# The remainder of a down product: one 96-row matmul per token tile and a last tile of 384 and 128 columns, in place of 32-row packing and a last tile of 256 and 256

## The chip, the cores and the metric

The kernel runs on one core of a Trainium2 chip. The metric is the device time of one execution in microseconds, lower is better. The time before is the median of three runs.

## What is computed

The kernel is a SwiGLU feed-forward layer in bf16:

```python
B, S, D, F = 1, 2048, 512, 1376
# x (B, S, D), w_gate (D, F), w_up (D, F), w_down (F, D)
def reference(x, w_gate, w_up, w_down):
    g = _silu(x @ w_gate)
    u = x @ w_up
    return (g * u) @ w_down
```

F is 1376 = 10 x 128 + 96. The hidden dimension is the contraction dimension of the down product, so each token tile needs ten full 128-row matmuls there and a remainder of 96 rows. That remainder is what the change is about.

## The kernel before

**Layout.** x is loaded transposed (xT_sb: D on partitions in KD = 4 blocks, tokens along the free dimension). The tokens are worked on in four chunks of 512 (NSC = 4), each of four tiles of 128 tokens (TPC = 4), sixteen tiles in all (NST = 16). The hidden activations hT_sb hold hidden rows on partitions, tokens along the free dimension, in NFF = 10 full blocks of 128 rows. PSUM is eight banks of 512 fp32 columns.

**Order of the work.** A small planner (`_Plan`) keeps one list of operations for each engine, in the order in which the code calls `op` and `dma`. Each operation names the operations that it depends on. At the end each list is written out, and a wait on a semaphore is put ahead of an operation where its dependency is on another engine; a wait for a count that the engine has already waited for is left out. A semaphore counts the finished operations of an engine, so waiting for one operation means waiting for all that stand before it in that engine's list. There is no other scheduling: each engine runs its list in order.

**Gate and up product (lines 172 to 194).** For every chunk and each of the ten full hidden blocks, TensorE does four matmuls for the gate into one of three banks (psG, banks 0 to 2) and four for up into one of two (psU, banks 3 and 4), all from `mm_k`, L172. ScalarE (ACT) takes the silu of the gate bank (L191), VectorE (DVE) multiplies it by the up bank and writes a 128 x 512 bf16 block of hT_sb (L194). `last_mult[c]` is the last such product of a chunk.

**The 96 remaining hidden rows** come in two blocks. Block X is one more set of four matmuls per chunk (also L172): its 128 output rows in bank 5 (psX) are the 96 gate rows and the last 32 up rows. ACT takes the silu of both parts (L222 and L223). Block Y is the first 64 up rows; it is done after all four chunks, two chunks side by side in the two column halves of the array (L232, 16 matmuls with a `tile_position`), into banks 6 and 7 (psY).

DVE then multiplies gate by up. Before the change this is done by `scatter` (L202): the 96 rows are cut into three groups of 32 rows (j) and each into four pieces of 128 tokens (r). Piece r goes to partitions 32r to 32r + 31 of hr_sb, so that the four token tiles of a chunk lie in four different 32-partition strips. Group 2 (from block X) is scattered chunk by chunk (`rest_x`), groups 0 and 1 (from block Y) after the last chunk (`rest_y`): 48 products of 32 x 128 in all, 32 of them at the end.

**Down product.** Chunks are taken in pairs. `main_pass` (L250) does the ten full matmuls of a token tile. `rest_pass` (L265) does the remainder of a whole chunk: for each of three groups, four matmuls of 32 rows, each in its own row strip of the array (`tile_position`) and into its own bank. The order on TensorE for a pair of chunks is: four main passes of the first chunk into banks 0 to 3, the rest pass of the first chunk (it closes those banks), the rest pass of the second chunk into banks 4 to 7 (it opens them), and four main passes of the second chunk. The 96 remainder rows of w_down are loaded four times, once to each strip (wdr_sb).

**Output.** `put` copies a bank to one of four o_sb buffers as bf16, on DVE (L284) or ACT (L282), and stores it (L286). The last of the sixteen tiles is done as two main passes of 256 columns (HD): the first in bank 7, copied by ACT and stored from ACT's queue, the second in bank 0, added by DVE to the part that the rest pass had left in bank 7 (part_sb, L300 and L279) and stored from SP's queue. All other stores and nearly all loads are issued by SP.

The first ten matmuls (L169) are there to warm TensorE up while the first loads arrive.

Of the kernel before, what the change touches and what calls it, by code (L numbers as in the profile page):

```python
# [4 lines left out]
ACT = mybir.ActivationFunctionType  # L5
ALU = mybir.AluOpType
BF16 = mybir.dt.bfloat16
# [11 lines left out]
class _Plan:  # L19
# [18 lines left out]
    def dma(self, eng, fn, deps=()):  # L38
        o = _Op(eng, fn, [d for d in deps if d is not None], False, self.sem(f"s_dma{self.n_dma}"))
        self.n_dma += 1  # L40
        self.lists[eng].append(o)
        return o
# [25 lines left out]
def bass_standalone__swiglu_ffn__prompt_kernel(nc, x, w_gate, w_up, w_down, out):  # L68
# [8 lines left out]
    NSC = S // SC  # L77
    TPC = SC // P
    NST = S // P
    HD = D // 2  # L80
    Q = 32
    assert D == 512 and S % SC == 0 and KD == 4 and TPC == 4 and F_LAST == 96 and NSC == 4

    xf = x[0]
# [7 lines left out]
    with ExitStack() as es:  # L92
# [3 lines left out]

        xT_sb = sb("xT_sb", [P, KD, S], BF16)
        w_sb = sb("w_sb", [P, KD, 2 * F], BF16)
        wd_sb = sb("wd_sb", [P, NFF, D], BF16)
        wdr_sb = sb("wdr_sb", [P, 3, D], BF16)  # L100
        hT_sb = sb("hT_sb", [P, NFF, S], BF16)
        hr_sb = sb("hr_sb", [P, 3, NSC, P], BF16)
        adummy = sb("act_dummy", [P, 8], FP32)
        NSG = 3
        sg_sb = [sb(f"sg_sb{i}", [P, SC], FP32) for i in range(NSG)]
        sgx_sb = [sb(f"sgx_sb{c}", [P, SC], FP32) for c in range(NSC)]
        sgy_sb = [sb(f"sgy_sb{c}", [P, SC], FP32) for c in range(NSC)]
        NOS = 4
        part_sb = sb("part_sb", [P, D], FP32)
        o_sb = [sb(f"o_sb{i}", [P, D], BF16) for i in range(NOS)]  # L110

        banks = [ps(f"bank{i}", [P, 512], FP32) for i in range(8)]
        NG, NU = 3, 2
        psG, psU, psX, psY = banks[0:3], banks[3:5], banks[5], banks[6:8]

        ones_w = nc.const_aps.tensor(1.0, [P, P], BF16)
        ones_m = nc.const_aps.tensor(1.0, [P, SC], BF16)
# [34 lines left out]
        for c in range(1, NSC):  # L152
            o = load_x("sp", c)
            for dk in range(KD):
# [1 line left out]
        got_wd = [  # L156
            dma("sp", lambda e: e.dma_start(
                wd_sb[:, 0:NFF, :], w_down[0:NFF * P, :].rearrange("(k p) d -> p k d", p=P))),
        ] + [
            dma("sp", lambda e, r=r: e.dma_start(  # L160
                wdr_sb[r * Q:(r + 1) * Q, :, :], w_down[NFF * P:F, :].rearrange("(j p) d -> p j d", p=Q)))
            for r in range(TPC)
        ]

        op("act", lambda e: e.activation(adummy[:, 0:4], zero_c, ACT.Silu), inc=False)  # L165
# [31 lines left out]
        def yblk(c):  # L197
            return (0, 64) if c % 2 == 0 else (64, 128)

        def scatter(c, j, sg, up, p0, deps):  # L200
            for r in range(TPC):
                o = op("dve", lambda e, r=r: e.tensor_tensor(  # L202
                    hr_sb[r * Q:(r + 1) * Q, j, c, :], sg[p0:p0 + Q, r * P:(r + 1) * P],
                    up[p0:p0 + Q, r * P:(r + 1) * P], ALU.mult), deps)
            return o

        n = 0
        rest_x, rest_a, last_mult = {}, {}, {}
        for c in range(NSC):
            ft0 = 0  # L210
            for ft in range(ft0, NFF):
                for dk in range(KD):
                    g = mm_g(n, c, ft, dk)
                for dk in range(KD):
                    u = mm_u(n, c, ft, dk)
                evac(n, c, ft, g, u)
                n += 1
            last_mult[c] = mults[-1]
            for dk in range(KD):
                xm = mm_k(psX, XC0, c, dk, [got_g[NFT - 1, dk], got_ut, rest_x.get(c - 1)])  # L220
            y0, y1 = yblk(c)
            op("act", lambda e, c=c: e.activation(sgx_sb[c][96:128, :], psX[64:96, :], ACT.Silu), [xm], inc=False)  # L222
            rest_a[c] = op("act", lambda e, c=c, y0=y0, y1=y1: e.activation(  # L223
                sgy_sb[c][y0:y1, :], psX[0:64, :], ACT.Silu), [xm])
            rest_x[c] = scatter(c, 2, sgx_sb[c], psX, 96, [rest_a[c]])

        rest_y = {}
        for pi in range(NSC // 2):
            for dk in range(KD):
                for c in (2 * pi, 2 * pi + 1):  # L230
                    y0, y1 = yblk(c)
                    ym = op("pe", lambda e, pi=pi, dk=dk, c=c, y0=y0, y1=y1: e.matmul(  # L232
                        psY[pi][y0:y1, :], lhsT=w_sb[:, dk, YC0:YC0 + 64], rhs=xT_sb[:, dk, c * SC:(c + 1) * SC],
                        start=(dk == 0), stop=(dk == KD - 1), tile_position=(0, y0), skip_group_check=True),
                        [got_u[NFT - 1, dk]], inc=(dk == KD - 1 and c % 2 == 1))
            for c in (2 * pi, 2 * pi + 1):
                y0, y1 = yblk(c)
                for j in range(2):
                    rest_y[c] = scatter(c, j, sgy_sb[c], psY[pi], y0 + j * Q, [rest_a[c], ym])


        stores = {}
        freed = {id(b): o for b, o in zip(banks, [[silus[-1]]] * NG + [[mults[-1]]] * NU + [[rest_x[NSC - 1]]] + [
            [rest_y[1]], [rest_y[NSC - 1]]])}

        def main_pass(t, bank, c0, ncol, opened):
            c = t // TPC
            for fk in range(NFF):
                deps = got_wd[0:1] + [last_mult[c]] + freed.get(id(bank), []) if fk == 0 else []
                om = op("pe", lambda e, fk=fk: e.matmul(  # L250
                    bank[:, c0:c0 + ncol],
                    lhsT=hT_sb[:, fk, t * P:(t + 1) * P], rhs=wd_sb[:, fk, c0:c0 + ncol],
                    start=(fk == 0 and not opened), stop=(fk == NFF - 1 and (opened or c0 > 0)), skip_group_check=True),
                    deps, inc=(fk == NFF - 1))
            return om

        def rest_pass(c, bank0, opening):
            for j in range(3):
                for r in range(TPC):
                    deps = []  # L260
                    if j == 0:
                        deps = got_wd[1:] + [rest_x[c], rest_y[c]]
                        if opening:
                            deps += freed.get(id(banks[bank0 + r]), [])
                    om = op("pe", lambda e, j=j, r=r: e.matmul(  # L265
                        banks[bank0 + r][:, :], lhsT=hr_sb[r * Q:(r + 1) * Q, j, c, :],
                        rhs=wdr_sb[r * Q:(r + 1) * Q, j, :], start=(opening and j == 0),
                        stop=(j == 2 and not opening), tile_position=(r * Q, 0), skip_group_check=True),
                        deps, inc=(j == 2 and r == TPC - 1))
            return om  # L270

        nout = 0

        def put(t, bank, c0, ncol, om, eng, q, part=None):
            nonlocal nout
            ob = o_sb[nout % NOS]
            prev = stores.get(nout - NOS, [])
            if part is not None:
                cp = op("dve", lambda e: e.tensor_tensor(  # L279
                    ob[:, c0:c0 + ncol], bank[:, c0:c0 + ncol], part_sb[:, c0:c0 + ncol], ALU.add), [om, part] + prev)  # L280
            elif eng == "act":
                cp = op("act", lambda e: e.activation(ob[:, c0:c0 + ncol], bank[:, c0:c0 + ncol], ACT.Copy), [om] + prev)  # L282
            else:
                cp = op("dve", lambda e: e.tensor_copy(ob[:, c0:c0 + ncol], bank[:, c0:c0 + ncol]), [om] + prev)  # L284
            freed.setdefault(id(bank), []).append(cp)
            stores.setdefault(nout, []).append(dma(q, lambda e: e.dma_start(  # L286
                of[t * P:(t + 1) * P, c0:c0 + ncol], ob[:, c0:c0 + ncol]), [cp]))
            if c0 + ncol == D:
                nout += 1

        for c in range(0, NSC, 2):
            for r in range(TPC):
                main_pass(c * TPC + r, banks[r], 0, D, False)
            om = rest_pass(c, 0, False)
            om2 = rest_pass(c + 1, TPC, True)
            for r in range(TPC):
                freed.pop(id(banks[r]), None)
                put(c * TPC + r, banks[r], 0, D, om, ("dve", "act")[r % 2], "sp")
            if c + 1 == NSC - 1:
                part = op("act", lambda e: e.activation(part_sb[:, HD:D], banks[7][:, HD:D], ACT.Copy), [om2])  # L300
            for r in range(TPC):
                t = (c + 1) * TPC + r
                bank = banks[TPC + r]
                freed.pop(id(bank), None)
                if t < NST - 1:
                    put(t, bank, 0, D, main_pass(t, bank, 0, D, True), "dve", "sp")
                else:
                    freed[id(bank)] = [part]
                    put(t, bank, 0, HD, main_pass(t, bank, 0, HD, True), "act", "act")
                    put(t, banks[0], HD, HD, main_pass(t, banks[0], HD, HD, False), "dve", "sp", part)  # L310
        for e in ("sp", "act"):
            plan.lists[e].append(_Op(e, None, [s for k in range(NST - NOS, NST) for s in stores[k] if s.eng == e], False))

        block = es.enter_context(nc.Block(no_gpsimd_drain=True))

# [43 lines left out]
```

## Time and profile before

| | us |
|---|---|
| median of 3 runs | 123.64 (123.58 to 123.75) |
| the profiled execution, its own time | 123.64 |
| its span, first to last instruction | 121.9 |
| TensorE matmul busy | 117.4 |
| DVE busy | 49.1 |
| ACT busy | 32.7 |
| granted TensorE clock (mean) | 1.000 |

The span is what the profile sees; what lies between it and the time of the execution is start and end of the program. Engines run side by side, so a busy time says what an engine did and not what set the end. A matmul's listed duration runs from its start to its modelled end, and matmuls overlap, so the pace of a stream has to be taken from the distance of starts. The loads are all in by about 28 us; the gate and up product runs to 78.2 us, block Y to 80.05 us, and the down product fills the rest.

### The profile page before, as it was taken

To read this page: it belongs to the slowest core of one execution; us is meant where nothing else is said; L and a number is where in the kernel's file an instruction comes from. 1 tells how busy PE (TensorE), PEld (TensorE's weight loads), DVE (VectorE), ACT (ScalarE), POOL (GpSimd) and SP (SyncE) were. 2 spreads that over 40 slices of the span, in tenths; PEclk is the share of its full clock that TensorE was granted. 3 is DMA by queue.
4 is the path that set the end of the run, shared out by engine and by line. 5 is a ranking of instruction groups with operands and counts; after the bars stand their busy time and mean duration, and the time that the engine had idled before them with its cause. 6 is when DMAs were issued, how large, how long until landed. Compare 5 with 4: busy or idle time off the path is not lost.

```text
span 121.9 us, 1487 instructions
## 1 busy us (share of the span) xinstructions
PE 117.4 (96%) x580; PEld 52.4 (43%) x580; DVE 49.1 (40%) x100; ACT 32.7 (27%) x56; POOL 0.2 (0%) x4
## 2 busy tenths in 40 slices
PE   7999999999999999999999999999969999999991
PEld 2244444444444444444444444444414444444470
DVE  0024433464433464424373443388893322004421
ACT  4033233353233353233443323400030000004010
POOL 0000000000000000000000000000000000000000
PEclk9999999999999999999999999999999999999999
DMA  4999999940000000000000000000005121003312
GB/s 85 253 285 375 263 231 264 337 85 0 0 0 0 0 0 5 0 0 5 0 0 0 0 0 0 5 0 0 0 0 172 48 86 43 0 0 113 102 53 76
DMA packets 18326, 8.80 MB, mean 72 GB/s; under 512 B 11408, under 2 KB 18320, under 8 KB 18320
## 3 DMA queue, kind: packets, MB, share of 16 engines
q1 hardware_dynamic: 17648, 8.52, 26.2%
q10 hardware_dynamic: 672, 0.20, 0.7%
q8 instruction: 4, 0.07, 0.2%
q14 instruction: 2, 0.02, 0.0%
HBM read 4.52 MB, written 2.10 MB: 54 GB/s over the span
## 4 chain that ended last, share of the span: by engine, by line
PE 87%; DVE 9%; issue 1%; ACT 1%
PE bank L172 60%; PE bank L250 21%; DVE hr_sb L202 8%; PE bank L169 4%; PE bank L265 2%; ACT sgy_sb L223 0%; ACT sgx_sb L222 0%; DVE o_sb L279 0%
## 5 line engine op out<-in xcount | busy, mean ns | idle before, releaser
L172 PE MATMUL bank<-xT_sb,w_sb 128*128 128x512 bf16 x336 | 73.1, 380 | 0.0
L172 PEld LDWEIGHTS bank<-xT_sb,w_sb 128*128 128x128 bf16 x336 | 32.9, 98 | 40.6 <-DMA xT_sb<-in_x_dram 0.9
L194 DVE TENSOR_TENSOR hT_sb<-sg_sb,bank 128x512 bf16<-128x512 f32 x40 | 27.5, 688 | 42.9 <-PE bank L172 42.8
L191 ACT ACTIVATE sg_sb<-bank 128x512 f32<-128x512 f32 x40 | 23.8, 596 | 43.9 <-PE bank L172 43.9
L250 PE MATMUL bank<-wd_sb,hT_sb 128*128 128x512 bf16 (+1 forms) x170 | 35.1, 367 | 0.0
L250 PEld LDWEIGHTS bank<-wd_sb,hT_sb 128*128 128x128 bf16 x170 | 16.3, 98 | 18.7 <-issue 1.3
L284 DVE CAST o_sb<-bank 128x512 bf16<-128x512 f32 x11 | 7.4, 690 | 19.5 <-PE bank L250 10.8
L282 ACT ACTIVATE o_sb<-bank 128x512 bf16<-128x512 f32 (+1 forms) x5 | 2.6, 552 | 36.3 <-PE bank L265 29.4
L202 DVE TENSOR_TENSOR hr_sb<-sgy_sb,bank 32x128 bf16<-32x128 f32 x32 | 9.1, 284 | 1.0
L202 DVE TENSOR_TENSOR hr_sb<-sgx_sb,bank 32x128 bf16<-32x128 f32 x16 | 4.7, 292 | 5.7 <-ACT sgy_sb L223 5.3
L169 PE MATMUL bank<-const-bfloat16-1.0 128*128 128x512 bf16 x10 | 4.4, 626 | 0.8 <-PEq L344 0.8
L265 PE MATMUL bank<-wdr_sb,hr_sb 32*128 32x512 bf16 x48 | 3.3, 377 | 1.1 <-DVE hr_sb L202 1.1
L222 ACT ACTIVATE sgx_sb<-bank 32x512 f32<-32x512 f32 x4 | 2.4, 588 | 4.5 <-PE bank L172 4.5
L169 PEld LDWEIGHTS bank<-const-bfloat16-1.0 128*128 128x128 bf16 x10 | 1.3, 138 | 3.0 <-issue 3.0
L265 PEld LDWEIGHTS bank<-wdr_sb,hr_sb 32*128 32x128 bf16 x48 | 1.1, 92 | 3.2 <-DVE hr_sb L202 1.6
L223 ACT ACTIVATE sgy_sb<-bank 64x512 f32<-64x512 f32 x4 | 2.4, 590 | 0.0
L232 PE MATMUL bank<-xT_sb,w_sb 128*64 128x512 bf16 x16 | 1.9, 382 | 0.0
L165 ACT ACT_TABLE_LOAD x1 | 1.3, 1283 | 1.2 <-PEq L344 1.2
L232 PEld LDWEIGHTS bank<-xT_sb,w_sb 128*64 128x64 bf16 x16 | 0.8, 109 | 1.0 <-issue 0.4
L279 DVE TENSOR_TENSOR o_sb<-bank,part_sb 128x256 bf16<-128x256 f32 x1 | 0.4, 425 | 1.5 <-PE bank L250 1.5
L300 ACT ACTIVATE part_sb<-bank 128x256 f32<-128x256 f32 x1 | 0.4, 390 | 0.0
L165 ACT ACTIVATE act_dummy<-const-float32-0.0 128x4 f32<-128x4 f32 x1 | 0.2, 205 | 0.0
(4 smaller groups left out, 0.4 us busy)
## 6 DMA issues: line engine op xcount, KB each, us to landing
out_dram<-o_sb SPq DMA_DIRECT2D x15, 128.0 KB, 1.8
wd_sb<-in_w_down_dram SPq DMA_DIRECT2D x1, 1280.0 KB, 9.0
w_sb<-in_w_gate_dram SPq DMA_DIRECT2D x1, 480.0 KB, 6.2
w_sb<-in_w_up_dram SPq DMA_DIRECT2D x1, 448.0 KB, 6.0
w_sb<-in_w_gate_dram SPq DMA_DIRECT2D x1, 384.0 KB, 4.9
w_sb<-in_w_up_dram SPq DMA_DIRECT2D x1, 384.0 KB, 5.4
wdr_sb<-in_w_down_dram SPq DMA_DIRECT2D x4, 96.0 KB, 7.0
w_sb<-in_w_up_dram SPq DMA_DIRECT2D x2, 128.0 KB, 3.4
```

Of the source, the lines that this page charges most:

```text
L169: op("pe", lambda e: e.matmul(banks[7][:, :], lhsT=ones_w, rhs=ones_m, start=True, stop=True), inc=False)
L172: return op("pe", lambda e: e.matmul(bank[:, :], lhsT=w_sb[:, dk, col0:col0 + P], rhs=xT_sb[:, dk, c * SC:(c + 1) * SC], start=(dk == 0), ...
L191: s = op("act", lambda e: e.activation(sg_sb[n % NSG][:, :], psG[n % NG][:, :], ACT.Silu), [g, mults[n - NSG] if n >= NSG else None])
L194: mults.append(op("dve", lambda e: e.tensor_tensor(hT_sb[:, ft, c * SC:(c + 1) * SC], sg_sb[n % NSG][:, :], psU[n % NU][:, :], ALU.mult), ...
L202: o = op("dve", lambda e, r=r: e.tensor_tensor(hr_sb[r * Q:(r + 1) * Q, j, c, :], sg[p0:p0 + Q, r * P:(r + 1) * P], up[p0:p0 + Q, r * P:(r ...
L222: op("act", lambda e, c=c: e.activation(sgx_sb[c][96:128, :], psX[64:96, :], ACT.Silu), [xm], inc=False)
L223: rest_a[c] = op("act", lambda e, c=c, y0=y0, y1=y1: e.activation(sgy_sb[c][y0:y1, :], psX[0:64, :], ACT.Silu), [xm])
L232: ym = op("pe", lambda e, pi=pi, dk=dk, c=c, y0=y0, y1=y1: e.matmul(psY[pi][y0:y1, :], lhsT=w_sb[:, dk, YC0:YC0 + 64], rhs=xT_sb[:, dk, c ...
L250: om = op("pe", lambda e, fk=fk: e.matmul(bank[:, c0:c0 + ncol], lhsT=hT_sb[:, fk, t * P:(t + 1) * P], rhs=wd_sb[:, fk, c0:c0 + ncol], sta ...
L265: om = op("pe", lambda e, j=j, r=r: e.matmul(banks[bank0 + r][:, :], lhsT=hr_sb[r * Q:(r + 1) * Q, j, c, :], rhs=wdr_sb[r * Q:(r + 1) * Q, ...
L282: cp = op("act", lambda e: e.activation(ob[:, c0:c0 + ncol], bank[:, c0:c0 + ncol], ACT.Copy), [om] + prev)
L284: cp = op("dve", lambda e: e.tensor_copy(ob[:, c0:c0 + ncol], bank[:, c0:c0 + ncol]), [om] + prev)
```

## The change

The 96 remaining rows get a block of their own in hT_sb and wd_sb (both now have eleven blocks), with 96 of the 128 partitions filled. `scatter`, hr_sb and wdr_sb are gone: block X's product is one DVE operation of 32 x 512 for each chunk, block Y's is one of 64 x 512. w_down's remainder is loaded once. The down product no longer goes in pairs of chunks: `down_group` does eleven matmuls for a tile, the eleventh with 96 rows and without a tile position, into banks 6 and 7 in turn, with its copy on DVE and its store on SP's queue, through three o_sb buffers. The last tile is two groups, of 384 and of 128 columns; the last of them is copied by ACT and stored from ACT's queue. Block Y's matmuls go to banks 0 and 1, and so wait for the last silu.

```diff
-        wd_sb = sb("wd_sb", [P, NFF, D], BF16)
-        wdr_sb = sb("wdr_sb", [P, 3, D], BF16)
-        hT_sb = sb("hT_sb", [P, NFF, S], BF16)
-        hr_sb = sb("hr_sb", [P, 3, NSC, P], BF16)
+        wd_sb = sb("wd_sb", [P, NFT, D], BF16)
+        hT_sb = sb("hT_sb", [P, NFT, S], BF16)
...
-        NOS = 4
-        part_sb = sb("part_sb", [P, D], FP32)
+        NOS = 3
...
-        NG, NU = 3, 2
-        psG, psU, psX, psY = banks[0:3], banks[3:5], banks[5], banks[6:8]
+        NG, NU, NO = 3, 2, 2
+        psG, psU, psX, psO, psY = banks[0:3], banks[3:5], banks[5], banks[6:8], banks[0:2]
...
-        ] + [
-            dma("sp", lambda e, r=r: e.dma_start(
-                wdr_sb[r * Q:(r + 1) * Q, :, :], w_down[NFF * P:F, :].rearrange("(j p) d -> p j d", p=Q)))
-            for r in range(TPC)
+            dma("sp", lambda e: e.dma_start(wd_sb[0:F_LAST, NFF, :], w_down[NFF * P:F, :])),
         ]
...
-            rest_x[c] = scatter(c, 2, sgx_sb[c], psX, 96, [rest_a[c]])
+            rest_x[c] = op("dve", lambda e, c=c: e.tensor_tensor(
+                hT_sb[64:96, NFF, c * SC:(c + 1) * SC], sgx_sb[c][96:128, :], psX[96:128, :], ALU.mult),
+                [rest_a[c]])
...
-                        [got_u[NFT - 1, dk]], inc=(dk == KD - 1 and c % 2 == 1))
+                        [got_u[NFT - 1, dk], silus[-1]], inc=(dk == KD - 1 and c % 2 == 1))
             for c in (2 * pi, 2 * pi + 1):
                 y0, y1 = yblk(c)
-                for j in range(2):
-                    rest_y[c] = scatter(c, j, sgy_sb[c], psY[pi], y0 + j * Q, [rest_a[c], ym])
+                rest_y[c] = op("dve", lambda e, pi=pi, c=c, y0=y0, y1=y1: e.tensor_tensor(
+                    hT_sb[0:64, NFF, c * SC:(c + 1) * SC], sgy_sb[c][y0:y1, :], psY[pi][y0:y1, :], ALU.mult),
+                    [rest_a[c], ym])
...
+        o_groups = [(t, 0, D) for t in range(NST - 1)] + [(NST - 1, 0, D - P), (NST - 1, D - P, P)]
+        NOG = len(o_groups)
+        freed, stores = [], {}
+
+        def down_group(gi, t, c0, ncol):
+            bank = psO[gi % NO]
             c = t // TPC
...
+            ob = o_sb[t % NOS]
+            for fk in range(NFT):
+                K = P if fk < NFF else F_LAST
+                deps = []
+                if fk == 0:
+                    deps += got_wd + [last_mult[c]] + (freed[gi - NO] if gi >= NO else [])
+                if fk == NFF:
+                    deps += [rest_x[c], rest_y[c]]
+                om = op("pe", lambda e, K=K, fk=fk: e.matmul(
+                    bank[:, 0:ncol], lhsT=hT_sb[0:K, fk, t * P:(t + 1) * P], rhs=wd_sb[0:K, fk, c0:c0 + ncol],
+                    start=(fk == 0), stop=(fk == NFT - 1)), deps, inc=(fk == NFT - 1))
+            deps = [om] + stores.get(t - NOS, [])
...
+            last = gi == NOG - 1
+            cps = [copy("act" if last else "dve", c0, c0 + ncol)]
+            store("act" if last else "sp", 0, P, cps)
+            freed.append(cps)
+
+        for gi, (t, c0, ncol) in enumerate(o_groups):
+            down_group(gi, t, c0, ncol)
```

The functions `scatter`, `main_pass`, `rest_pass` and `put` and the loop over pairs of chunks, printed above, are removed as a whole.

More of the change, by code (lines that the diff above doesn't have):

```diff
@@ L79, in bass_standalone__swiglu_ffn__prompt_kernel @@
     NST = S // P
-    HD = D // 2
-    Q = 32
     assert D == 512 and S % SC == 0 and KD == 4 and TPC == 4 and F_LAST == 96 and NSC == 4
@@ L198, in yblk @@
             return (0, 64) if c % 2 == 0 else (64, 128)
[L200 to L205, printed above, removed]
         n = 0
@@ L234, in bass_standalone__swiglu_ffn__prompt_kernel @@
                         start=(dk == 0), stop=(dk == KD - 1), tile_position=(0, y0), skip_group_check=True),
-                        [got_u[NFT - 1, dk]], inc=(dk == KD - 1 and c % 2 == 1))
+                        [got_u[NFT - 1, dk], silus[-1]], inc=(dk == KD - 1 and c % 2 == 1))
             for c in (2 * pi, 2 * pi + 1):
                 y0, y1 = yblk(c)
-                for j in range(2):
-                    rest_y[c] = scatter(c, j, sgy_sb[c], psY[pi], y0 + j * Q, [rest_a[c], ym])
-        stores = {}
@@ L243, in bass_standalone__swiglu_ffn__prompt_kernel @@
-        freed = {id(b): o for b, o in zip(banks, [[silus[-1]]] * NG + [[mults[-1]]] * NU + [[rest_x[NSC - 1]]] + [
-            [rest_y[1]], [rest_y[NSC - 1]]])}
-        def main_pass(t, bank, c0, ncol, opened):
-            c = t // TPC
[L248 to L310, printed above, removed]
+                rest_y[c] = op("dve", lambda e, pi=pi, c=c, y0=y0, y1=y1: e.tensor_tensor(
+                    hT_sb[0:64, NFF, c * SC:(c + 1) * SC], sgy_sb[c][y0:y1, :], psY[pi][y0:y1, :], ALU.mult),
+                    [rest_a[c], ym])
@@ new lines, in bass_standalone__swiglu_ffn__prompt_kernel, with copy, store @@
+        o_groups = [(t, 0, D) for t in range(NST - 1)] + [(NST - 1, 0, D - P), (NST - 1, D - P, P)]
[3 more added lines that the diff above has]
+            bank = psO[gi % NO]
+            c = t // TPC
+            ob = o_sb[t % NOS]
[10 more added lines that the diff above has]
+            deps = [om] + stores.get(t - NOS, [])
+            def copy(eng, a, b):
+                if eng == "act":
+                    return op("act", lambda e: e.activation(ob[:, a:b], bank[:, a - c0:b - c0], ACT.Copy), deps)
+                return op("dve", lambda e: e.tensor_copy(ob[:, a:b], bank[:, a - c0:b - c0]), deps)
+            def store(eng, p0, p1, after):
+                r0 = t * P
+                stores.setdefault(t, []).append(dma(eng, lambda e: e.dma_start(
+                    of[r0 + p0:r0 + p1, c0:c0 + ncol], ob[p0:p1, c0:c0 + ncol]), after))
+            last = gi == NOG - 1
+            cps = [copy("act" if last else "dve", c0, c0 + ncol)]
+            store("act" if last else "sp", 0, P, cps)
+            freed.append(cps)
@@ L311, in bass_standalone__swiglu_ffn__prompt_kernel @@
+        for gi, (t, c0, ncol) in enumerate(o_groups):
+            down_group(gi, t, c0, ncol)
         for e in ("sp", "act"):
-            plan.lists[e].append(_Op(e, None, [s for k in range(NST - NOS, NST) for s in stores[k] if s.eng == e], False))
+            plan.lists[e].append(_Op(e, None, [s for t in range(NST - NOS, NST) for s in stores[t] if s.eng == e], False))
         block = es.enter_context(nc.Block(no_gpsimd_drain=True))
```

## The prediction

> **What bounds the kernel now.** I read the page first (engine totals and the chain that ended last), then the timeline around the joint of the two products, then the timeline of the end, and then the groups by shape, for prices. From the page, TensorE's row and the lines of the chain:
>
> ```profile
> PE 117.4 (96%) x580; PEld 52.4 (43%) x580; DVE 49.1 (40%) x100; ACT 32.7 (27%) x56; POOL 0.2 (0%) x4
> PE 87%; DVE 9%; issue 1%; ACT 1%
> PE bank L172 60%; PE bank L250 21%; DVE hr_sb L202 8%; PE bank L169 4%; PE bank L265 2%; ACT sgy_sb L223 0%; ACT sgx_sb L222 0%; DVE o_sb L279 0%
> ```
>
> TensorE is busy for 96% of the span, but 8% of the chain is the scatter L202 on DVE. So in one place the end is set by DVE and not by TensorE. The timeline from 74 to 95 us shows the place (start, length, engine, line, operation):
>
> ```profile
> 78.20 1.92 PE L232 MATMUL bank<-xT_sb,w_sb 128*64 128x512 bf16 x16
> 79.52 1.26 DVE L202 TENSOR_TENSOR hr_sb<-sgx_sb,bank 32x128 bf16<-32x128 f32 x4 [1.33 <-ACT sgy_sb L223]
> 80.05 8.81 PE L250 MATMUL bank<-wd_sb,hT_sb 128*128 128x512 bf16 x40
> 80.81 10.06 DVE L202 TENSOR_TENSOR hr_sb<-sgy_sb,bank 32x128 bf16<-32x128 f32 x32
> 88.79 1.04 PE L265 MATMUL bank<-wdr_sb,hr_sb 32*128 32x512 bf16 x15
> 90.93 0.82 PE L265 MATMUL bank<-wdr_sb,hr_sb 32*128 32x512 bf16 x9 [1.10 <-DVE hr_sb L202]
> ```
>
> The 32 small products run to 80.81 + 10.06 = 90.87. The second packed pass needs those of chunk 1; they come after those of chunk 0 on DVE, and a semaphore count makes the pass wait. TensorE stops in the middle of L265 until 90.93. Later nothing interrupts it (timeline from 91.4 to 111, then the end from the timeline of 100 to 122):
>
> ```profile
> 91.68 17.44 PE L250 MATMUL bank<-wd_sb,hT_sb 128*128 128x512 bf16 x80
> 109.05 1.47 PE L265 MATMUL bank<-wdr_sb,hr_sb 32*128 32x512 bf16 x24
> ```
> ```profile
> 110.46 8.83 PE L250 MATMUL bank<-wd_sb,hT_sb 128*128 128x512 bf16 x50
> 118.23 0.38 ACT L282 ACTIVATE o_sb<-bank 128x256 bf16<-128x256 f32 x1 [6.94 <-PE bank L250]
> 118.65 0.37 ACTq L286 DMA_DIRECT2D out_dram<-o_sb  x1
> 119.33 0.42 DVE L279 TENSOR_TENSOR o_sb<-bank,part_sb 128x256 bf16<-128x256 f32 x1 [1.49 <-PE bank L250]
> ```
>
> The matmuls end at 110.46 + 8.83 = 119.29; an add, a store and its landing carry the rest to 121.9. The prices come from the groups by shape (between the bars: busy us, mean ns of one) and the page's store rows (us to landing):
>
> ```profile
> L194 DVE TENSOR_TENSOR hT_sb<-sg_sb,bank 128x512 bf16<-128x512 f32 x40 | 27.5, 688 | 42.9 <-PE bank L172 42.8
> L250 PE MATMUL bank<-wd_sb,hT_sb 128*128 128x512 bf16 x150 | 32.9, 379 | 0.0
> L250 PE MATMUL bank<-wd_sb,hT_sb 128*128 128x256 bf16 x20 | 2.3, 272 | 0.0
> L282 ACT ACTIVATE o_sb<-bank 128x512 bf16<-128x512 f32 x4 | 2.2, 594 | 29.4 <-PE bank L265 29.4
> L282 ACT ACTIVATE o_sb<-bank 128x256 bf16<-128x256 f32 x1 | 0.4, 384 | 6.9 <-PE bank L250 6.9
> ```
> ```profile
> out_dram<-o_sb SPq DMA_DIRECT2D x15, 128.0 KB, 1.8
> out_dram<-o_sb ACTq DMA_DIRECT2D x1, 64.0 KB, 1.6
> out_dram<-o_sb SPq DMA_DIRECT2D x1, 64.0 KB, 1.5
> ```
>
> **The pace of matmuls.** A matmul's 379 ns overlaps the next, so the pace is taken from starts. From 80.05 to 88.79 there are 40 (8.74 us), from 91.68 to 109.05 there are 80 (17.37 us); each stretch ends in one change of array mode. The difference, 40 matmuls in 8.63 us, gives 0.2158 us each, and what is left, 8.74 - 8.63 = 0.11 us, is the price of one change of mode. In the end stretch 30 matmuls of 512 columns take 6.47 us, to 116.93; the last one starts at 119.29 - 0.27 = 119.02, so 19 steps of 256 columns take 2.09 us, 0.110 each. On the line through both, 384 columns cost 0.163 and 128 cost 0.057; by the same line through 379 and 272 ns, a lone 128-column matmul lasts 0.218.
>
> **What the change removes on TensorE.** The first pair of packed passes goes with its stall: 91.68 - 88.79 = 2.89 us. The second: 110.46 - 109.05 = 1.41. Each pair has also a change of mode ahead of it, 2 x 0.11. Together 4.52 us. Without the stall the two would be 2.82 + 0.22, so the stall is 2.89 - 1.41 = 1.48 of it.
>
> **What it adds on TensorE.** Every token tile gets an eleventh matmul of 96 rows: 15 of 512 columns, and one 384 and one 128 wide, 15 x 0.2158 + 0.22 = 3.46 us. Splitting the last tile 384 + 128 instead of 256 + 256 leaves its other matmuls at 10 x (0.163 + 0.057) = 2.20, as 20 x 0.110. Only its very last matmul ends sooner after its start (0.218 against 0.272). Net: 4.52 - 3.46 + 0.05, about 1.1 us less. Built up from the front: the down product still starts at 80.05, takes 165 x 0.2158 = 35.60, then 11 x 0.163 = 1.79, 10 steps of 0.057 and 0.22 for the last, and ends at 118.23, against 119.29.
>
> So the packing itself was worth 3.46 - 3.04 = 0.42 us to the kernel before, and its wait cost 1.48: the change gives up the first and gets back the second. A rule speaks against that. The Trainium skill, "TensorE: Matmul & The Clock Gate", Part 3, says that a 32-row matmul takes as long as a 128-row one and that four packed tiles were measured 3.07 times as fast. By its 3.07 the 48 small matmuls would cost 3.4 us, nearly the 3.46 that the 16 full ones cost; the trace has them cheaper, at 2 x 1.41.
>
> Three prices here are not in the trace. (1) A 96-row matmul: the rows have 128 (L250) and 32 (L265). A step is columns, since both take 0.216 us per set of 512 columns (24 packed in four lanes, 6 sets, in 1.41 less 0.11), so I take 0.2158. It can't stream faster than that; it is dearer only if 96 rows set another array mode, which is the first rival. The code gives these matmuls no tile position, unlike L232 and L265, so I take no change of mode. (2) A 128-column step: 0.057 from the line, at most 0.098, the weight load's own row (L250 PEld, 98 ns), if loads cease to overlap; the 256-column row (0.110, at its streaming pace) is nearest, so 0.057, and up to 0.41 us more in the range. The same page, Back-to-back issue gap, has 81 ns a matmul sustained at 128 columns; by that the sum would be 0.24 us longer. (3) The new DVE products are 32 and 64 partitions wide. DVE's rows go by columns (284 ns for 128, 688 for 512), and on ACT 32 and 64 partitions (588, 590) cost what 128 do (596); I take 0.69, at worst 4 x 0.284 = 1.14, what the four pieces cost before.
>
> **What moves to other engines, and what hides it.** DVE has 48 products less (13.8 us) and 12 of 0.69 more (8.3 us). In chunks 0 to 2 that is 0.69 for 1.26 us, in DVE's idle time. At the joint: ACT's L223 ends at 79.5; the product of block X runs to 80.21, the Y products to 80.9, 81.6, 82.3 and 83.0. TensorE needs the first of these only at the eleventh matmul of the first tile, 80.05 + 2.16 = 82.21: 1.3 us of cover. With the cover gone TensorE would wait for DVE, the second rival. Copies: all full tiles go to DVE, 0.69 in every 2.37 us, and two banks alternate. The first tile ends at 82.6; its copy, queued behind the Y products, runs from 83.0 to 83.7, and the third tile needs the bank at 84.8. Later copies have over 1.6 us. ACT loses four copies that cost nothing.
>
> The Y matmuls move to banks 0 and 1 and wait for the last silu. It started at 76.58 and takes 0.60, and L232 starts at 78.20, 1.0 us later; only the down product is behind it on TensorE. The down banks 6 and 7 are then free of the first product. Loads: one of 96 rows in place of four on SP's queue; all land before 28 us, first used at 80.05. Stores go out every 2.37 us, land in 1.8 and have three buffers (7.1 us): no wait.
>
> **The end.** Last matmul 118.23; ACT starts 0.04 later (as 119.33 against 119.29) and copies 128 columns in 384 - 105 = 0.28 us; 0.04 to the store on its own queue (118.61 to 118.65): 118.59. Landing 1.6: 120.19. Before, the store went out at 119.78, landed at 121.28, and the span closed 0.6 later. That gives a span of 120.8. The other part is not later: the 384-column group ends at 117.60, its copy lasts (0.69 + 0.42) / 2 = 0.56, its store leaves at 118.2 and lands by 119.7 to 120.0. The profiled execution took 123.64 us, which is the median, so 1.74 lie outside the span, and the forecast is 120.8 + 1.74, 122.5 us. What is late next is TensorE itself, unbroken.
>
> The store of 128 columns writes rows of 256 B, which no row has: 1.5 at best (the 64 KB row), and at worst 2.8, the longest landing of L286, when five stores were in flight. I take 1.6, the nearest, since only one store is before it.
>
> **Rivals.**
> 1. *Mode changes, slower.* The eleventh matmul sets another array mode in each of 17 groups, twice per group: 34 x 0.11 = 3.7 us, 126.2 us. For: no 96-row matmul is in the trace, and each of the six changes there costs about that. Against: no tile position is given. From 0.033 us a change it eats the gain; from 0.04 the kernel is slower by over 0.2%. Chance 0.07.
> 2. *The wait moves and stays.* DVE's products are late for the first tile, as if it waited for all four: 83.0 instead of 82.21, 0.8 us, 123.3. Against: the count it waits for is that of the first. Chance 0.04.
> 3. *The narrow end costs.* Steps at 0.098 (+0.41) and a slow landing (up to +1.2): 122.9, at the far end 124.1. For: stores to DRAM in 256 B pieces are new. Against: one store alone. Chance 0.07.
> 4. *Forecast*: stall gone, packing given up, 122.5. Chance 0.82; its own range is 122.2 (end 0.3 shorter: a landing of 1.5 and a shorter closing on ACT) to 122.9.
>
> **Numbers.** A measurement of this kernel can tell 0.2% (0.25 us) from no change. Faster: the forecast, most of rivals 2 and 3, 0.88. Same: their upper part, 0.03. Slower: rival 1 and the far end of 3, 0.09. The range runs from 122.2 to 123.1, leaving out rival 1, half of 2 and half of 3.
>
> **What would show it.** In the changed profile DVE's hr_sb vanishes from the chain, and the down product is one TensorE stretch of about 38.2 us from 80.05 with no idle time named DVE; the eleventh matmul is labelled 128 rows or starts 0.216 after the tenth (right) or 0.32 (rival 1). A DVE wait near 82 us is rival 2; last matmuls 0.1 apart, or a landing over 2 us on ACT's queue, rival 3. A first product that no longer ends at 78.2, or gaps between tiles, would make the prediction wrong in a way not named.

## The result and the profile after

The changed kernel takes 122.19 us (median of four runs, 121.95 to 122.68), against 123.63 for the kernel before in the same comparison: a ratio of 0.9887, 95% interval 0.9853 to 0.9922. That is 1.1% faster, with the interval clear of 1; the median lies 0.3 us below the forecast of 122.5 and 0.01 below the lower end of the range.

Its profiled execution took 121.95 us, with a span of 120.2 us. The chain of its page, by engine and by line:

```profile
PE 94%; DMA 4%; ACT 0%; issue 0%
PE bank L164 61%; PE bank L245 32%; DMA xT_sb<-in_x_dram 4%; PE bank L219 2%; ACT o_sb L252 0%
```

DVE is no longer in the chain; before, its scatter held 8% of it. L245 is the down product, L164 the gate and up product, L219 block Y. The 4% of DMA are the first x load: in this profile the warm-up matmuls ended at 4.71 us and TensorE then waited for that load until 5.05; before, they lasted to 5.20 and the product followed at once. The timeline from 74 to 90 us, at the joint where TensorE stood still before:

```profile
77.79 1.92 PE L219 MATMUL bank<-xT_sb,w_sb 128*64 128x512 bf16 x16
79.64 10.55 PE L245 MATMUL bank<-wd_sb,hT_sb 128*128 128x512 bf16 x48
79.84 2.83 DVE L225 TENSOR_TENSOR hT_sb<-sgy_sb,bank 64x512 bf16<-64x512 f32 x4
82.70 0.69 DVE L253 CAST o_sb<-bank 128x512 bf16<-128x512 f32 x1
```

No TensorE row here has a wait behind it. The four Y products take 2.83 us where 32 small ones took 10.06, and the first copy queues behind them, as foretold, without delaying anyone. The chain from 76 us on shows the whole down product as one piece, and the timeline of the end shows what follows it:

```profile
79.71 38.21 PE bank L245 x187
```
```profile
117.32 0.56 DVE L253 CAST o_sb<-bank 128x384 bf16<-128x384 f32 x1 [1.10 <-PE bank L245]
117.94 0.28 ACT L252 ACTIVATE o_sb<-bank 128x128 bf16<-128x128 f32 x1 [38.85 <-PE bank L245]
118.24 0.36 ACTq L257 DMA_DIRECT2D out_dram<-o_sb  x1
```

The difference of the two profiles splits into three stretches. The table gives them for all the kernels of this study, worked out from the starts in each trace: when block Y begins (so, how late the gate and up product is), from there to the end of the last matmul, and from there to the end of the span. "Stretch" below means the middle one; the expectations count from the first down matmul, 1.85 us less where no wait stands before it.

| profile | Y begins | Y and down product | end |
|---|---|---|---|
| before | 78.20 | 41.09 | 2.57 |
| changed | 77.79 | 40.11 | 2.27 |
| changed, second profile (after_again) | 78.55 | 40.11 | 2.27 |
| free_bank7 | 77.81 | 39.61 | 2.56 |
| tail_256_256 | 78.64 | 40.11 | 2.46 |
| packed_free_narrow | 77.84 | 39.61 | 2.38 |
| chunk1_first | 77.97 | 41.09 | 2.58 |
| rows_128 | 78.06 | 40.04 | 2.27 |
| y_in_down_banks | 77.93 | 41.85 | 2.28 |
| one_full_between | 78.12 | 40.47 | 2.58 |

Of the 1.69 us between the first two rows, 0.98 are in the down product, 0.30 at the end, and 0.41 came before block Y, where the change alters no matmul (after_again, below, takes that up).

### The profile page after: what moved, and what is told of

It is laid out like the page before. It is cut to its first block, busy times and chain, and to the rows that moved or that the text cites. A ratio compares the mean times of both kernels' runs of the same rounds, so it can differ in the third digit from the quotient of the medians.

```text
span 120.2 us, 1381 instructions
## 1 busy us (share of the span) xinstructions
PE 116.8 (97%) x549; PEld 52.6 (44%) x549; DVE 44.0 (37%) x64; ACT 30.1 (25%) x51; POOL 0.2 (0%) x4
## 4 chain that ended last, share of the span: by engine, by line
PE 94%; DMA 4%; ACT 0%; issue 0%
PE bank L164 61%; PE bank L245 32%; DMA xT_sb<-in_x_dram 4%; PE bank L219 2%; ACT o_sb L252 0%
## 5 line engine op out<-in xcount | busy, mean ns | idle before, releaser
L164 PE MATMUL bank<-xT_sb,w_sb 128*128 128x512 bf16 x336 | 72.8, 379 | 0.3 <-DMA xT_sb<-in_x_dram 0.3
L164 PEld LDWEIGHTS bank<-xT_sb,w_sb 128*128 128x128 bf16 x336 | 32.7, 98 | 40.5 <-DMA xT_sb<-in_x_dram 0.8
L245 PE MATMUL bank<-wd_sb,hT_sb 128*128 128x512 bf16 (+4 forms) x187 | 38.3, 366 | 0.0
L245 PEld LDWEIGHTS bank<-wd_sb,hT_sb 128*128 128x128 bf16 (+1 forms) x187 | 17.8, 98 | 20.7 <-issue 0.4
L253 DVE CAST o_sb<-bank 128x512 bf16<-128x512 f32 (+1 forms) x16 | 10.9, 683 | 24.3 <-PE bank L245 24.2
L161 PE MATMUL bank<-const-bfloat16-1.0 128*128 128x512 bf16 x10 | 3.9, 572 | 0.8 <-PEq L300 0.8
L210 DVE TENSOR_TENSOR hT_sb<-sgx_sb,bank 32x512 bf16<-32x512 f32 x4 | 2.8, 692 | 4.9 <-ACT sgy_sb L208 4.9
L225 DVE TENSOR_TENSOR hT_sb<-sgy_sb,bank 64x512 bf16<-64x512 f32 x4 | 2.7, 684 | 0.1
L219 PE MATMUL bank<-xT_sb,w_sb 128*64 128x512 bf16 x16 | 1.9, 382 | 0.0
L219 PEld LDWEIGHTS bank<-xT_sb,w_sb 128*64 128x64 bf16 x16 | 0.8, 109 | 1.0 <-issue 0.4
L300 POOL MEMSET const-bfloat16-1.0<- 128x1 bf16 x1 | 0.1, 102 | 0.0
L300 POOL MEMSET const-uint8-127<- 128x1 uint8 x1 | 0.1, 102 | 0.0
L300 POOL MEMSET const-float32-0.0<- 128x1 f32 x1 | 0.1, 99 | 0.2 <-issue 0.2
L300 POOL MEMSET const-float32-1.0<- 128x1 f32 x1 | 0.1, 99 | 0.0
```

Source lines behind the costliest of these rows:

```text
L161: op("pe", lambda e: e.matmul(banks[7][:, :], lhsT=ones_w, rhs=ones_m, start=True, stop=True), inc=False)
L164: return op("pe", lambda e: e.matmul(bank[:, :], lhsT=w_sb[:, dk, col0:col0 + P], rhs=xT_sb[:, dk, c * SC:(c + 1) * SC], start=(dk == 0), ...
L210: rest_x[c] = op("dve", lambda e, c=c: e.tensor_tensor(hT_sb[64:96, NFF, c * SC:(c + 1) * SC], sgx_sb[c][96:128, :], psX[96:128, :], ALU.m ...
L225: rest_y[c] = op("dve", lambda e, pi=pi, c=c, y0=y0, y1=y1: e.tensor_tensor(hT_sb[0:64, NFF, c * SC:(c + 1) * SC], sgy_sb[c][y0:y1, :], ps ...
L245: om = op("pe", lambda e, K=K, fk=fk: e.matmul(bank[:, 0:ncol], lhsT=hT_sb[0:K, fk, t * P:(t + 1) * P], rhs=wd_sb[0:K, fk, c0:c0 + ncol], ...
L253: return op("dve", lambda e: e.tensor_copy(ob[:, a:b], bank[:, a - c0:b - c0]), deps)
```

## The experiments

**The start: after_again.** The changed kernel, unedited.

> The changed kernel once more, unedited, for the spread of its time and a second look at its start. Theory A (what its first profile shows beyond the prediction, 0.4 us, is the start: the full clock came 1.9 us earlier there than in the profile of the kernel before, and this falls differently from run to run): runs spread over about 0.7 us, and in each profile the gate and up product ends the earlier, between 77.7 and 78.5 us, the earlier the full clock comes; the down product takes 38.2 to 38.3 us whatever the start. Rival B (the new kernel starts faster by construction): the product ends at 77.8 in every profile, and the time stays near 122.0.

Measured: 122.35 us, six runs from 121.93 to 122.72; ratio 0.9896 (0.9869 to 0.9924). The profile is of the slowest of them. The down product took the same time to the nearest 0.01 us, and block Y began 0.76 us later than in the first profile. The warm-up matmuls show why; groups by shape of the first profile and then of this one (between the bars: busy us, mean ns of one):

```profile
L161 PE MATMUL bank<-const-bfloat16-1.0 128*128 128x512 bf16 x10 | 3.9, 572 | 0.8 <-PEq L300 0.8
```
```profile
L161 PE MATMUL bank<-const-bfloat16-1.0 128*128 128x512 bf16 x10 | 4.4, 629 | 0.8 <-PEq L300 0.8
```

The first line is that of the first profile. There the granted clock became full at 4.08 us, by the trace's clock record, and the last warm-up matmuls already ran at it: they start 0.43 us apart at first and 0.21 apart from 4.12 us on. In the second it became full at 6.50 us, so that three matmuls of the product ran at about half pace (starts 366 to 427 ns apart in place of 216), on top of an x load that released the product 0.3 us later. The kernel before had 6.00 us in its profile. It isn't the clock alone: rows_128 had its clock at 4.06 us, but its product was released by x 0.19 us later than in the first profile and waited 0.09 us longer for a w load, and block Y began at 78.06. The Trainium skill, "TensorE: Matmul & The Clock Gate", Part 1, says that the window which opens the clock runs free of the kernel, so that the moment differs from run to run. These profiles agree that it moves, but over 2.9 us (3.79 to 6.69), more than the 500 ns either way that the page gives. Rival B falls: the five profiles with the changed down product have block Y begin between 77.79 and 78.64 us, the five with the old one between 77.81 and 78.20, so nothing in the change makes the start faster. Without the 0.41 us the change is worth 1.28 us, which would put the profiled 123.64 at 122.36, about the median here.

**What TensorE waited for: free_bank7.** The kernel before, with the bank of chunks 2 and 3 copied out by ACT:

```diff
+        ycp_sb = sb("ycp_sb", [P, SC], FP32)
...
+            ysrc, ydep = psY[pi], ym
+            if pi == 1:
+                ysrc = ycp_sb
+                ydep = ycopy = op("act", lambda e: e.activation(ycp_sb[:, :], psY[1][:, :], ACT.Copy), [ym])
...
-                    rest_y[c] = scatter(c, j, sgy_sb[c], psY[pi], y0 + j * Q, [rest_a[c], ym])
+                    rest_y[c] = scatter(c, j, sgy_sb[c], ysrc, y0 + j * Q, [rest_a[c], ydep])
...
-            [rest_y[1]], [rest_y[NSC - 1]]])}
+            [rest_y[1]], [ycopy]])}
```

> The kernel before with one edit: ACT copies the second Y bank (bank 7, chunks 2 and 3) to SBUF, and the small products of chunks 2 and 3 read that copy; the packing stays. Theory A (the 1.48 us stall is the wait for bank 7, which the products of chunks 2 and 3 hold until 90.87): the copy ends near 80.7, the 24 packed matmuls run in 1.41 without a break, and the time falls by 1.5 us to about 122.15. Theory B, as the prediction put it (the pass waits for the products of chunk 1): those are unchanged, and so is the time, 123.6.

Measured: 121.84 us (121.77 to 121.95), ratio 0.9866 (0.9843 to 0.9889). The timeline from 76 to 95 us:

```profile
79.77 0.60 ACT L240 ACTIVATE ycp_sb<-bank 128x512 f32<-128x512 f32 x1 [0.66 <-PE bank L233]
80.43 5.01 DVE L203 TENSOR_TENSOR hr_sb<-sgy_sb,bank 32x128 bf16<-32x128 f32 x16
85.47 5.00 DVE L203 TENSOR_TENSOR hr_sb<-sgy_sb,ycp_sb 32x128 bf16<-32x128 f32 x16
88.40 0.98 PEld L270 LDWEIGHTS bank<-wdr_sb,hr_sb 32*128 32x128 bf16 x24 [0.42 <-issue]
88.40 1.47 PE L270 MATMUL bank<-wdr_sb,hr_sb 32*128 32x512 bf16 x24
```

All 24 packed matmuls now run in one piece at 88.40, although DVE is busy with the last 16 products until 90.47 as before. The stretch falls from 41.09 to 39.61, by 1.48 us, which is the stall. The products of chunk 1 were ready at 85.44 in this profile and can't have been what the pass waited for. The bank was.

**The same question from the other side: chunk1_first.**

```diff
-            for c in (2 * pi, 2 * pi + 1):
+            for c in ((1, 0) if pi == 0 else (2, 3)):
...
-            [rest_y[1]], [rest_y[NSC - 1]]])}
+            [rest_y[0]], [rest_y[NSC - 1]]])}
```

> The kernel before with the small Y products of chunk 1 ahead of those of chunk 0; nothing else moves, and bank 7 is still read until the end. Theory B (the packed pass of chunk 1 waits for its own products): they are done some 2.5 us sooner, the stall of 1.48 us shrinks or goes, and the time falls towards 122. Theory A (it waits for bank 7, which the products of chunks 2 and 3 hold until about 90.9): the break stays behind the fifteenth packed matmul with 1.48 us, the down stretch stays at 39.24 us, and the time at 123.4 to 123.6.

Measured: 123.44 us, ratio 1.0 (0.9974 to 1.0026), stretch 41.09: no change. Timeline from 76 to 95 us:

```profile
80.59 10.05 DVE L202 TENSOR_TENSOR hr_sb<-sgy_sb,bank 32x128 bf16<-32x128 f32 x32
88.56 1.04 PE L265 MATMUL bank<-wdr_sb,hr_sb 32*128 32x512 bf16 x15
90.70 0.82 PE L265 MATMUL bank<-wdr_sb,hr_sb 32*128 32x512 bf16 x9 [1.10 <-DVE hr_sb L202]
```

The break stands behind the fifteenth packed matmul again: twelve of the first pass and three of the second, for banks 4, 5 and 6. The sixteenth would open bank 7.

**The same mechanism in the changed kernel: y_in_down_banks.**

```diff
-        psG, psU, psX, psO, psY = banks[0:3], banks[3:5], banks[5], banks[6:8], banks[0:2]
+        psG, psU, psX, psO, psY = banks[0:3], banks[3:5], banks[5], banks[6:8], banks[6:8]
...
-                    deps += got_wd + [last_mult[c]] + (freed[gi - NO] if gi >= NO else [])
+                    deps += got_wd + [last_mult[c]] + (freed[gi - NO] if gi >= NO else [rest_y[2 * gi + 1]])
```

> The changed kernel with the Y matmuls back in banks 6 and 7, where the first two token tiles then have to wait for the products that read them. Theory A (a bank held by products is what costs): TensorE can start the first tile only after the product of chunk 1, at about 1.6 us after the last Y matmul is issued, and the second needs no further wait; the down product starts 1.6 us later and the time is 1.6 us longer, about 123.9. Theory B (bank release plays no part): no change, 122.3.

Measured: 123.87 us (123.73 to 124.52), ratio to the kernel before 1.0036 (1.0006 to 1.0067). The gain is gone. Timeline from 77 to 88 us:

```profile
79.98 2.83 DVE L225 TENSOR_TENSOR hT_sb<-sgy_sb,bank 64x512 bf16<-64x512 f32 x4
81.52 6.64 PE L245 MATMUL bank<-wd_sb,hT_sb 128*128 128x512 bf16 x30 [1.68 <-DVE hT_sb L225]
```

TensorE starts the down product when the second of the four products is done, and then runs on. The stretch is 1.74 us longer than the changed kernel's; 1.6 was expected. So the small edit of psY's banks in the diff carries more than the whole gain: with wide products, the same order of tiles and the old banks for Y the kernel is not faster.

**The price of a 96-row matmul: rows_128.**

```diff
+        op("dve", lambda e: e.memset(hT_sb[F_LAST:P, NFF, :], 0.0))
+        op("dve", lambda e: e.memset(wd_sb[F_LAST:P, NFF, :], 0.0))
...
-                K = P if fk < NFF else F_LAST
+                K = P
```

> The changed kernel with the eleventh matmul on all 128 rows; the 32 added rows of both operands are set to zero by DVE before the first product, so the result is the same. Theory A (a 96-row matmul costs 5 ns on entry and 3 ns on leaving, as the starts of the changed kernel show): 17 groups lose 0.12 us, the down stretch is 38.14 instead of 38.26, and the time at equal starts falls by 0.1 us, less than run-to-run spread. Rival B (the eleventh matmul is dear for another reason, its wait or its new bank): the stretch stays at 38.26.

Measured: 122.19 us (122.13 to 122.40); the stretch fell by 0.07 us, not by 0.12. The down product in the chain of this kernel (from 79 us on) and, again, of the changed one (from 76):

```profile
79.98 38.13 PE bank L247 x187
```
```profile
79.71 38.21 PE bank L245 x187
```

A 96-row matmul among 128-row ones costs about 4 ns (0.07 over 17 groups), against 216 for the matmul itself. The matmul behind it starts 220 ns later and the next one 218 to 219, in place of 215 to 216. The expected 0.12 counted both; it left out that the other starts of the changed kernel lie slightly closer than those of rows_128 (more of them 215 than 216 ns apart), so the sum is 0.07.

**The narrow end: tail_256_256.**

```diff
-        o_groups = [(t, 0, D) for t in range(NST - 1)] + [(NST - 1, 0, D - P), (NST - 1, D - P, P)]
+        o_groups = [(t, 0, D) for t in range(NST - 1)] + [(NST - 1, 0, D // 2), (NST - 1, D // 2, D // 2)]
```

> The changed kernel with its last tile back at 256 and 256 columns. Theory A (the narrow last group saves 0.05 us of the last matmul and 0.11 us of ACT's copy): 0.15 us slower than the changed kernel, about 122.35, with the down stretch 0.05 longer and the last copy 384 ns. Rival B (the narrow store's 256 B rows cost as much as the narrow copy saves): no slower.

Measured: 122.29 us (122.16 to 123.00), ratio 0.9915 (0.9887 to 0.9944). Against the changed kernel's 122.35 the medians decide nothing, since the starts differ by more than the effect. The stretches do: the end grew by 0.19 us, from 2.27 to 2.46, while the matmuls took just as long (the expected 0.05 in them did not come). Timeline of the end:

```profile
118.78 0.38 ACT L252 ACTIVATE o_sb<-bank 128x256 bf16<-128x256 f32 x1 [38.85 <-PE bank L245]
119.20 0.36 ACTq L257 DMA_DIRECT2D out_dram<-o_sb  x1
```

The last stores of the two profiles, this one's first (us to landing at the end):

```profile
out_dram<-o_sb ACTq DMA_DIRECT2D x1, 64.0 KB, 1.6
```
```profile
out_dram<-o_sb ACTq DMA_DIRECT2D x1, 32.0 KB, 1.5
```

Copying 256 columns takes 0.38 us and 128 take 0.28; most of the other 0.09 is in the landing (1.55 against 1.48 in the traces). For a single store as this one, rival B, dear 256-byte pieces, falls.

**The price of a change of mode: one_full_between.** On top of free_bank7:

```diff
+            op("pe", lambda e: e.matmul(banks[TPC][:, :], lhsT=ones_w, rhs=ones_m, start=True, stop=True),
+               freed.get(id(banks[TPC]), []), inc=False)
             om2 = rest_pass(c + 1, TPC, True)
```

> The kernel with bank 7 copied out, and one extra full-array matmul of 512 columns between the two packed passes of each pair of chunks, so that the array changes mode twice more per pair; its product is cleared by the next matmul. Theory A (a change of mode costs 0.105 us): the down stretch grows from 37.76 by 2 x (0.216 + 0.21) to 38.6 us. Rival B (the gap is the cost of starting a packed pass, not of the change): it grows by the matmuls alone, 0.43, to 38.2.

Measured: the stretch grew by 0.87 us (a single run, 122.99 us in all). Two matmuls are 0.43 of it, so the four added changes, from strips to the whole array and back, cost 0.43 us, 0.108 each. The chain from 79 to 120 us, the first pair of passes:

```profile
88.78 0.76 PE bank L270 x12
89.53 0.32 PE bank L300
89.86 0.76 PE bank L270 x12
```

The lone full matmul, L300, holds TensorE 0.32 us in place of 0.216. At this price rival 1 of the prediction would have cost what it said; it didn't come, since rows_128 finds 4 ns at a 96-row matmul and no such gap.

**A better version: packed_free_narrow.** free_bank7 with its last tile 384 and 128 wide:

```diff
-    HD = D // 2
+    HD = D - P
...
-                    put(t, banks[0], HD, HD, main_pass(t, banks[0], HD, HD, False), "dve", "sp", part)
+                    put(t, banks[0], HD, D - HD, main_pass(t, banks[0], HD, D - HD, False), "dve", "sp", part)
```

> The kernel before with bank 7 copied out by ACT and its last tile 384 and 128 wide: packing kept, stall gone, short end. Theory A (packing was worth 0.42 us more than one 96-row matmul per tile, and only the wait made the old kernel slower): 123.63 less 1.48 for the stall and 0.18 for the end, 122.0, and with equal starts 0.3 to 0.5 us faster than the changed kernel. Rival B (packed passes cost as much as the full-width ones once all is counted): level with the changed kernel.

Measured: 121.71 us (121.58 to 121.83), ratio to the kernel before 0.9853 (0.9827 to 0.9880): the fastest here, each of its runs below each of the changed kernel's in the same comparison. From block Y on it is 0.40 us faster than the changed kernel (41.98 against 42.38): 0.50 in the down product, 0.11 given back at the end. Timeline of its end:

```profile
116.92 0.49 ACT L287 ACTIVATE o_sb<-bank 128x384 bf16<-128x384 f32 x1 [7.58 <-PE bank L255]
117.48 0.29 DVE L284 TENSOR_TENSOR o_sb<-bank,part_sb 128x128 bf16<-128x128 f32 x1 [1.49 <-PE bank L255]
```

The add fell from 0.42 to 0.29 us, and the end from 2.56 to 2.38. The new rival B, that packed passes are no cheaper, falls.

## Why the prediction was right, and where it was not

**The removal.** The stall was priced at 1.48 us and the packing's worth at 0.42. free_bank7 takes only the stall away and falls by 1.48. The changed kernel, which also gives up the packing, lies 0.50 above free_bank7; 0.07 of that are the 96 rows, and the 0.43 left are the 0.42. The skill's 3.07, cited there, was the poorer guide: without the mode changes, 24 packed matmuls take 1.41 - 0.11 = 1.30 us for 5.18 us of single ones, four times as fast and not 3.07.

**The cause of the stall was read wrongly.** The prediction said that the pass waits for the products of chunk 1, queued behind those of chunk 0. The size didn't depend on it, but the reading was wrong: chunk1_first shows that their order doesn't matter, and free_bank7 that with bank 7 released there is no stall. The lines shown in the prediction had the answer. At their pace, 32 products in 10.06 us, those of chunk 1 were done near 85.8 us, 3 us before the packed passes began. And the break came after fifteen matmuls and not after twelve, so the second pass had begun; only the strip that opens bank 7 waited, until the last product had read it. That the stall went as a whole is owed to the move of block Y to banks 0 and 1, which the prediction mentions and does not price; with Y left in banks 6 and 7, y_in_down_banks is 1.74 us slower, and the prediction's reading of the stall gives no reason for that.

**The added matmuls.** From the first start to the last end the down product took 38.26 us (39.24 before), against 38.18 by the prediction's sum. The 96-row steps were taken as free of a surcharge; they cost 0.07 together, nearly all of the difference. The 128-column steps were drawn out to 0.057 and came at 0.055 to 0.058. The Trainium skill, "TensorE: Matmul & The Clock Gate", Back-to-back issue gap, has 81 ns sustained at this width; here the weight loads, listed at 98 ns each, started 55 to 58 ns apart and overlapped one another, and the lower figure held. The term of 0.05 for a sooner end of the very last matmul, in the difference sum, doesn't exist: it starts later by as much (tail_256_256, 40.11 for both). The sum from the front, which gave 1.06 and not 1.1, was the right one; 0.98 was measured.

**The cover.** All of it held: no wait of TensorE behind DVE, ACT or a store after 79.64 us. The products ended at 82.67, against 83.0 at a joint foreseen 0.41 later, so 0.1 later against the joint itself. TensorE needed the first of them at 81.81 and had it at 80.52.

**The end was mis-sized.** Predicted 2.57 us from the last matmul to the end of the span (118.23 to 120.8), as before the change; measured 2.27. Copy (0.28) and hand-over came as worked out. The landing took 1.5 and not the 1.6 taken (1.48 in the trace), and the program closed 0.45 us later, not 0.6. The other traces show the same split: 0.44 to 0.46 wherever the last store is ACT's, 0.53 to 0.56 wherever it is SP's. The prediction had named both as the lower end of its own range. So the forecast gave 1.06 us for the down product and nothing for the end, and 0.98 and 0.30 came; it is the end that puts the mechanism's 1.28 above the forecast gain of 1.1.

**The start** has no term in the prediction. The first profile's 0.41 us came from it and drops out of the mechanism; the first median, 122.19, lies just below the range and the second, 122.35, inside it, which fits the luck of the start and is no part of the mechanism. All ten runs of the changed kernel lie between 121.93 and 122.72. The two that were profiled, 121.95 and 122.72, are 0.77 apart, of which 0.76 is the start; the others have no profile, so for them this isn't shown.

**The rivals.** Mode changes (1) and the narrow end (3) didn't come; their prices were tested, 0.108 us a change and a landing of 1.5. The moved wait (2) didn't come in the form described, but y_in_down_banks shows that a bank, not a late product, would have brought it, at 1.74 us.

## What to carry to other kernels

Where a matmul waits for another engine in the middle of a group, count the instructions that ran ahead of the break: they tell which bank or operand is awaited, and the cheapest cure may be to copy that one bank out early, not to restructure the work. A change that bundles a cure with a giving-up is best split: here the cure, with the packing kept and the short end added, beats the change by 0.4 us. When runs differ by as much as the effect, compare the stretches of the trace that the change touches, not the totals.

## What the runs showed that was not expected

What stopped TensorE was a bank held by slow readers, not the operand of the next pass: one ACT copy of 0.60 us gave back 1.48 us. Row packing in four strips reached the full factor of four in the middle of a stream, as the trace before had it, and each change between packed and full mode cost 0.108 us. A 96-row matmul among 128-row ones costs about 4 ns extra. The full clock came between 3.79 and 6.69 us after the start, and the gate and up product, the same in all these kernels, ended over a range of 0.85 us.
